# First tokens by quarters of the FFN units, with partial sums in SBUF; attention's element work on VectorE and ScalarE

## The chip, the core and the metric

The kernel runs on one core of one Trainium2 chip. The metric is the device time of one execution in microseconds; the runs' median is compared, and one execution was profiled.

## The reference, cut to what matters

An RWKV attention over batch 4, 8 heads, 768 steps, 48 channels a head; its output, as 3072 tokens of 384 features, goes through an RMS norm and a two-layer gated FFN with 1536 units:

```python
for t in range(S):
    cur = np.einsum('bhd,bhe->bhde', u[None] * kt, vt)
    y[:, :, t] = np.einsum('bhd,bhde->bhe', rt, state + cur)
    state = w[None, :, :, None] * state + np.einsum('bhd,bhe->bhde', kt, vt)
...
xn = x / rms * rms_g
g = xn @ w_gate
silu = g * (1.0 / (1.0 + np.exp(-g)))
return (silu * (xn @ w_val) @ w_out).astype(np.float32)
```

The three weight matrices come as 64-bit floats.

## The kernel before

The 768 steps are cut into 12 chunks of 64 steps; a chunk holds all four sequences, so 256 tokens. For each chunk `mixing` makes the attention: `prep` (L279 to L290) scales r and k into ME, MO and kc, multiplies r, k and u into rk, sums that to du and writes du on the diagonals of ME and MO; `prep_k` (L301) scales k into KH for the state; `scores` (L314) multiplies within the chunk and copies under a mask (L319); `states` (L371) and `outputs` (L337, L342) follow; `normalise` (L388 to L393) makes xT from yT and the sum sq of its squares (L350 to L355). rk, KH, the diagonals and the sums of sq are GpSimd's.

The FFN works on blocks of chunks, `blocks = [[0], [1], [2, 3], [4, 5], ...]`: products are 256 columns wide in the first two and 512 after. The 1536 units are 12 groups of 128, called units here (the index `nn`). `gate_val` multiplies a unit's gate and value weights with xT into two PSUM banks (L408), takes the sigmoid on ScalarE (L413) and two products on VectorE (L414, L415) to make h. `project` (L422) multiplies, for 128 tokens at a time, the h of all 12 units with w_out into one PSUM tile and ScalarE copies it out (L426).

The weights come in 24 pieces of 128x576. `stage` loads a raw piece (three buffers); `round_piece` makes the rounded 32-bit piece: one pass on ScalarE (ulp, L184), four on VectorE (mag, L186 to L191), of which L186 and L187 clamp small magnitudes, and an addition on GpSimd (L194). Pieces go in the order of all gate and value quarters, then all of w_out; a quarter is three units. `rounded(n)` makes a step wait in program order until n pieces are done.

The program is written as steps of the FFN with steps of the next block's mixing spread between them, and a scheduler then fixes one list per engine; each engine works through its list in order. All loads and stores are issued by SyncE (SP). At the end a count of decay values in range is read, and another, general path is taken if one was out of range.

## Time and profile before

| what | us |
|---|---|
| median of three runs | 766.51 (764.3 to 767.57) |
| the profiled execution's own time | 763.99 |
| its span, first to last instruction | 761.7 |
| TensorE busy in the span | 680.2 |
| VectorE, GpSimd, ScalarE busy | 338.9, 220.3, 154.9 |

The profile gives, for each engine, the busy time of its instructions. Engines work side by side, so the numbers don't add up to the span; what counts is which engine the others wait for in each stretch. PE is TensorE, DVE VectorE, ACT ScalarE, POOL GpSimd.

### The profile page before, as it was taken

The numbers are of one execution on the slowest core, as the hardware profiler recorded it, in microseconds if no ns is written. First come the engines' busy times: TensorE is split into PE (matmuls) and PEld (weight loads), VectorE is DVE, ScalarE is ACT, GpSimd is POOL, SyncE is SP. The second block draws the span as 40 slices with busy tenths as digits, with TensorE's granted clock in tenths as the row PEclk, the third lists the DMA queues.
The fourth block names the chain that finished last, engine by engine and source line by source line (L and its number), as shares of the span: only waits on it lengthen the run. The fifth ranks groups of instructions, "written<-read, shape, count | busy, mean of one in ns | idle before, by whom it ended". The sixth has DMA issues, their size and how long they took to land.

```text
span 761.7 us, 9960 instructions
## 1 busy us (share of the span) xinstructions
PE 680.2 (89%) x4238; PEld 389.6 (51%) x4238; DVE 338.9 (44%) x435; ACT 154.9 (20%) x307; POOL 220.3 (29%) x141
## 2 busy tenths in 40 slices
PE   2465667788999999999999999999999999999994
...
GB/s 230 169 49 163 236 76 197 130 42 78 100 41 30 16 75 53 99 11 42 72 8 52 99 11 42 78 0 64 100 0 1 1 1 22 22 0 0 1 21 27
DMA packets 13639, 46.85 MB, mean 62 GB/s; under 512 B 3216, under 2 KB 6288, under 8 KB 12432
## 3 DMA queue, kind: packets, MB, share of 16 engines
...
## 4 chain that ended last, share of the span: by engine, by line
PE 66%; POOL 13%; DVE 13%; issue 3%; DMA 3%; ACT 1%; POOLq 0%; ACTq 0%; DVEq 0%
PE pg L408 21%; PE pv L408 20%; PE po L422 17%; POOL KH L301 4%; DMA TOK<-in_tok_dram 3%; DVE xT L393 3%; PE pa L314 2%; PE pu L371 2%; POOL rk L285 2%; POOL rk L286 2%; DVE mag L191 2%; DVE mag L186 2%; PE py L337 1%; DVE mag L187 1%; PE py L342 1%
## 5 line engine op out<-in xcount | busy, mean ns | idle before, releaser
L408 PE MATMUL pg<-xT,wg 128*128 128x512 f32 (+1 forms) x504 | 210.6, 552 | 14.3 <-POOL wg L194 8.8
L408 PE MATMUL pv<-xT,wv 128*128 128x512 f32 (+1 forms) x504 | 203.4, 540 | 12.9 <-POOL wv L194 12.9
L422 PE MATMUL po<-wo,h 128*128 128x384 f32 x576 | 195.6, 495 | 12.3 <-POOL wo L194 10.3
L422 PEld LDWEIGHTS po<-wo,h 128*128 128x128 f32 x576 | 107.6, 191 | 87.0 <-POOL wo L194 12.6
L408 PEld LDWEIGHTS pv<-xT,wv 128*128 128x128 f32 x504 | 97.1, 194 | 104.6 <-issue 85.4
L408 PEld LDWEIGHTS pg<-xT,wg 128*128 128x128 f32 x504 | 96.6, 197 | 99.9 <-issue 69.4
L301 POOL TENSOR_TENSOR KH<-TOK,wk 64x768 f32<-64x768 f32 x22 | 47.0, 2137 | 244.0 <-PE pu L371 243.2
L414 DVE TENSOR_TENSOR h<-pg,h 128x512 f32<-128x512 f32 (+1 forms) x84 | 51.4, 612 | 145.1 <-ACT h L413 144.9
L413 ACT ACTIVATE h<-pg 128x512 f32<-128x512 f32 (+1 forms) x84 | 45.0, 536 | 287.7 <-PE pg L408 286.5
L415 DVE TENSOR_TENSOR h<-pv,h 128x512 f32<-128x512 f32 (+1 forms) x84 | 51.5, 613 | 70.0 <-PE pv L408 69.0
L426 ACT COPY o<-po 128x384 f32<-128x384 f32 x24 | 11.5, 478 | 194.5 <-PE po L422 140.7
L280 DVE TENSOR_TENSOR ME<-chan,up 48x1024 f32<-48x1024 f32 x12 | 18.5, 1543 | 61.1 <-PE py L342 61.1
L354 POOL TENSOR_TENSOR sq<-sq 128x256 f32<-128x256 f32 x12 | 17.0, 1419 | 89.6 <-ACT sq L350 89.6
L314 PE MATMUL pa<-ME,kc 48*64 48x64 f32 x384 | 30.3, 231 | 12.5 <-DVE kc L279 12.5
L314 PEld LDWEIGHTS pa<-ME,kc 48*64 48x64 f32 x384 | 26.3, 143 | 28.3 <-issue 13.8
L337 PE MATMUL py<-ME,VS 128*64 128x64 f32 x288 | 36.7, 231 | 2.5 <-DVE ME L319 2.0
L337 PE MATMUL py<-MO,VS 128*64 128x64 f32 x288 | 36.7, 231 | 1.5 <-DVE MO L319 1.5
L288 DVE TENSOR_REDUCE du<-rk 128x16 f32<-128x768 f32 x12 | 11.4, 951 | 57.0 <-POOL rk L286 57.0
L391 DVE RECIPROCAL rms<-rms 128x256 f32<-128x256 f32 x12 | 21.0, 1746 | 34.7 <-ACT rms L390 34.7
L342 PE MATMUL py<-MO,VS 128*48 128x64 f32 x288 | 36.2, 227 | 0.0
L342 PE MATMUL py<-ME,VS 128*48 128x64 f32 x288 | 36.2, 227 | 0.0
L393 DVE SCALAR_TENSOR_TENSOR xT<-yT,gcol,rms 128x256 f32<-128x256 f32 x36 | 33.4, 977 | 0.4
...
## 6 DMA issues: line engine op xcount, KB each, us to landing
...
raw<-in_wgt_dram SPq DMA_DIRECT2D x8, 576.0 KB, 4.1
raw<-in_wvl_dram SPq DMA_DIRECT2D x8, 576.0 KB, 4.5
raw<-in_wot_dram SPq DMA_DIRECT2D x8, 576.0 KB, 4.3
...
```

The lines of the kernel that those rows point to most:

```text
L280: nc.vector.tensor_mul(me[0:D], ch[0:D, 0], table(up[0:D]))
L301: nc.gpsimd.tensor_mul(KH[rows, z], TOK[rows, 1], free_dims(wk[rows], (0, B), (D, HP), (1, D)))
L314: nc.tensor.matmul(pa[to, bl, p, :], kc[rows, b, p, :], m[rows, b, p, :], start=True, stop=True, skip_group_check=True,)
L337: nc.tensor.matmul(py[64 * z : 64 * z + 64, i, cols], vs[:, z, b, at : at + L], m[:, b, 3, :], start=True, stop=False, skip_group_check=True,)
L342: nc.tensor.matmul(py[64 * z : 64 * z + D, i, cols], vs[:, z, b, i * D : (i + 1) * D], m[:, b, i, :], start=False, stop=True, skip_group_c ...
L391: nc.vector.reciprocal(rms, rms)
L393: nc.vector.scalar_tensor_tensor(out=xT[:, i, at : at + B * L], in0=yT_of[s][:, i], scalar=gcol[:, i : i + 1], in1=rms, op0=ALU.mult, op1= ...
L408: nc.tensor.matmul(ps_, wt[:, cc, o * P : (o + 1) * P], xT[:, cc, 0:nt], start=cc == 0, stop=cc == CC - 1)
L413: nc.scalar.activation(h, pg, AF.Sigmoid)
L414: nc.vector.tensor_mul(h, pg, h)
L415: nc.vector.tensor_mul(h, pv, h)
L422: nc.tensor.matmul(po, hT[blk, nn][:, j * P : (j + 1) * P], wo[i][:, o, :], start=nn == 0, stop=nn == NN - 1)
```

## The change

Chunks 0 to 3 go through the FFN one by one (256 columns), and chunks 0 to 2 by quarters: `cell(q, s)` makes units 3q to 3q+2 of chunk s and multiplies their h with that quarter of w_out. The first quarter's result is copied to SBUF by ScalarE, the later ones are added to it by VectorE. The pieces are ordered quarter by quarter, gate, value, out. From chunk 4 on there are blocks of two chunks as before. Attention's products rk, KH and the sums of sq are made by VectorE, the diagonals by 32 small ScalarE operations a chunk (chunk 0: four VectorE operations), and MO's lower half is a ScalarE copy of ME; ME and MO have one buffer instead of two. The PSUM pool `ps_at` has two banks instead of three, `ps_o` two instead of one. The clamp of small weights is gone from `round_piece`; instead `checks` loads every piece a second time and counts small magnitudes with two ScalarE passes, and the count decides on the general path at the end, together with the decay count.

```diff
-    ps_at = ctx.enter_context(tc.tile_pool(name="ps_at", bufs=3, space=PSUM))
-    ps_o = ctx.enter_context(tc.tile_pool(name="ps_o", bufs=1, space=PSUM))
+    ps_at = ctx.enter_context(tc.tile_pool(name="ps_at", bufs=2, space=PSUM))
+    ps_o = ctx.enter_context(tc.tile_pool(name="ps_o", bufs=2, space=PSUM))
...
+    ME = c_tile([P, B, HP, L], "ME")
+    MO = c_tile([P, B, HP, L], "MO")
...
+    pieces = [
+        (dst[i], src[i], k) for i in range(WQ) for dst, src in ((wg, wgt), (wv, wvl), (wo, wot)) for k in range(2)
+    ]
+    PER_Q = len(pieces) // WQ
+    queue, staged, state = deque(pieces), deque(), {"done": 0}
...
-            mag = raws.tile([P, CUT], FP32, name=f"mag_{n}", tag="mag", bufs=2)
+            bits = raws.tile([P, CUT], I32, name=f"bits_{n}", tag="bits", bufs=2)
             ulp = raws.tile([P, CUT], I32, name=f"ulp_{n}", tag="ulp", bufs=2)
             nc.scalar.activation(ulp, lo, AF.Copy, scale=2.0**-29)
-            mi = mag.bitcast(I32)
-            nc.vector.tensor_single_scalar(out=mi, in_=hi, scalar=0x7FFFFFFF, op=ALU.bitwise_and)
-            nc.vector.tensor_single_scalar(out=mag, in_=mag, scalar=2.0**-15, op=ALU.max)
             nc.vector.tensor_scalar(
-                out=mi, in0=mi, scalar1=3, scalar2=0x3FFFFFF8, op0=ALU.logical_shift_left, op1=ALU.bitwise_and
+                out=bits, in0=hi, scalar1=3, scalar2=0x3FFFFFF8, op0=ALU.logical_shift_left, op1=ALU.bitwise_and
             )
             nc.vector.scalar_tensor_tensor(
-                out=mi, in0=hi, scalar=-0x40000000, in1=mi, op0=ALU.bitwise_and, op1=ALU.bitwise_or
-            )
-            nc.gpsimd.tensor_tensor(out=dst.bitcast(I32), in0=mi, in1=ulp, op=ALU.add)
+                out=bits, in0=hi, scalar=-0x40000000, in1=bits, op0=ALU.bitwise_and, op1=ALU.bitwise_or
+            )
+            nc.gpsimd.tensor_tensor(out=dst.bitcast(I32), in0=bits, in1=ulp, op=ALU.add)
...
+    def checks(n):
+        _, src, k = pieces[n]
+        raw = raws.tile([P, CUT], I64, name=f"again_{n}", tag="raw")
+        nc.sync.dma_start(out=raw, in_=src[:, k * CUT : (k + 1) * CUT])
+        hi = raw.bitcast(I32).rearrange("p (n z) -> p n z", z=2)[:, :, 1].bitcast(FP32)
+        mag = raws.tile([P, CUT], FP32, name=f"mag_{n}", tag="ulp", bufs=2)
+        nc.scalar.activation(mag, hi, AF.Abs)
+        nc.scalar.activation(mag, mag, AF.Relu, scale=-(2.0**15), bias=1.0, accum_out=seen[:, n : n + 1])
...
-        nc.vector.tensor_mul(kc, ch[:, 1], table(down))
-        nc.vector.tensor_mul(me[0:D], ch[0:D, 0], table(up[0:D]))
-        nc.vector.tensor_mul(mo[64 : 64 + D], ch[64 : 64 + D, 0], table(up[64 : 64 + D]))
+        nc.vector.tensor_mul(ME, CH[:, 0], table(up))
+        nc.scalar.copy(MO[64:128], ME[64:128])
+        nc.vector.tensor_mul(kc, CH[:, 1], table(down))
         if s + 1 < NS:
             load_chan(s + 1)
+    def prep_u(s):
         rk = one.tile([P, B, HP, D], FP32, name=f"rk_{s}", tag="rk")
-        nc.gpsimd.tensor_mul(rk, TOK[:, 0], TOK[:, 1])
-        nc.gpsimd.tensor_mul(rk, rk, free_dims(utab, (0, B), (D, HP), (1, D)))
+        nc.vector.tensor_mul(rk, TOK[:, 0], TOK[:, 1])
+        nc.vector.tensor_mul(rk, rk, free_dims(utab, (0, B), (D, HP), (1, D)))
         du = work.tile([P, B * HP], FP32, name=f"du_{s}", tag="du")
         nc.vector.tensor_reduce(out=du, in_=rk.rearrange("p b h d -> p (b h) d"), op=ALU.add, axis=AX.X)
-        for t, rows in ((me, slice(64, 128)), (mo, slice(0, 64))):
-            nc.gpsimd.tensor_mul(
-                t[rows].rearrange("p b h t -> p (b h) t"),
-                free_dims(dmask[rows], (0, B * HP), (1, L)),
-                free_dims(du[rows], (1, B * HP), (0, L)),
-            )
+        for half in range(2):
+            for t, rows in ((ME, slice(64, 128)), (MO, slice(0, 64))):
+                if s == 0:
+                    nc.vector.tensor_mul(
+                        t[rows, 2 * half : 2 * half + 2].rearrange("p b h t -> p (b h) t"),
+                        free_dims(dmask[rows], (0, 2 * HP), (1, L)),
+                        free_dims(du[rows, 2 * HP * half :], (1, 2 * HP), (0, L)),
+                    )
+                    continue
+                for b in (2 * half, 2 * half + 1):
+                    for p in range(HP):
+                        x = b * HP + p
+                        nc.scalar.mul(t[rows, b, p, :], dmask[rows], du[rows, x : x + 1])
...
-            nc.gpsimd.tensor_mul(
+            nc.vector.tensor_mul(
                 KH[rows, z], TOK[rows, 1], free_dims(wk[rows], (0, B), (D, HP), (1, D))
...
-            nc.gpsimd.tensor_add(sq[:, 0], sq[:, 0], sq[:, 1])
-            nc.gpsimd.tensor_add(sq[:, 0], sq[:, 0], sq[:, 2])
+            nc.vector.tensor_add(sq[:, 0], sq[:, 0], sq[:, 1])
+            nc.vector.tensor_add(sq[:, 0], sq[:, 0], sq[:, 2])
...
+    def mixing(s, blk, at):
+        def last():
+            if at == 0:
+                xTs[blk] = work.tile([P, CC, 512], FP32, name=f"xT_{blk}", tag="xT", bufs=3)
+            normalise(s, xTs[blk], at)
+        def fourth():
+            outputs(s, 1)
+            states(s, 0)
+            states(s, 1)
+            if s + 2 < NS:
+                load_v(s + 2)
+        return [
+            lambda: prep_r(s), lambda: (prep_u(s), prep_k(s)), lambda: scores(s, 0), lambda: scores(s, 1),
+            lambda: outputs(s, 0), fourth, last,
+        ]
...
+    def project(blk, j, s, units, part=None):
+        rounded(PER_Q * ((units[-1]) // NQ + 1))
+        name = f"{blk}_{j}_{units[0]}"
+        po = ps_o.tile([P, DM], FP32, name=f"po_{name}", tag="po")
+        for nn in units:
             i, o = divmod(nn, NQ)
             nc.tensor.matmul(
-                po, hT[blk, nn][:, j * P : (j + 1) * P], wo[i][:, o, :], start=nn == 0, stop=nn == NN - 1
-            )
-        osb = work.tile([P, DM], FP32, name=f"o_{blk}_{j}", tag="o")
-        nc.scalar.copy(osb, po)
-        for bl in range(2):
-            row = (2 * (j % 2) + bl) * S + s * L
-            nc.sync.dma_start(out=out[row : row + L, :], in_=osb[bl * L : (bl + 1) * L, :])
-    blocks = [[0], [1]] + [[s, s + 1] for s in range(2, NS, 2)]
-    xTs = {}
-    def mixing(s, blk, at):
-        def first():
-            prep(s)
-            prep_k(s)
-        def third():
-            states(s, 0)
-            outputs(s, 0)
-        def fourth():
-            states(s, 1)
-            outputs(s, 1)
-            if s + 2 < NS:
-                load_v(s + 2)
-        def fifth():
-            if at == 0:
-                xTs[blk] = work.tile([P, CC, 512], FP32, name=f"xT_{blk}", tag="xT")
-            normalise(s, xTs[blk], at)
-        return [first, lambda: scores(s, 0), lambda: scores(s, 1), third, fourth, fifth]
-    load_v(1)
-    for f in mixing(0, 0, 0):
-        f()
-        round_piece()
-    for blk, chunks in enumerate(blocks):
-        nt = len(chunks) * B * L
-        ffn = [lambda nn=nn: gate_val(blk, nn, xTs[blk], nt) for nn in range(NN)]
-        ffn += [lambda j=j: project(blk, j, chunks[j // 2]) for j in range(nt // P)]
-        mix = []
-        if blk + 1 < len(blocks):
-            for x, s in enumerate(blocks[blk + 1]):
-                mix += mixing(s, blk + 1, x * B * L)
-        todo = deque(mix)
-        for x, f in enumerate(ffn):
+                po, hT[blk, nn][:, j * P : (j + 1) * P], wo[i][:, o, :], start=nn == units[0], stop=nn == units[-1]
+            )
+        if part in (None, 0):
+            osb = sums[blk, j] = work.tile([P, DM], FP32, name=f"o_{name}", tag="o", bufs=2 * FIRST)
+            nc.scalar.copy(osb, po)
+        else:
+            osb = sums[blk, j]
+            nc.vector.tensor_add(osb, po, osb)
...
+    def cell(q, s):
+        units = list(range(q * NQ, (q + 1) * NQ))
+        return [lambda nn=nn: gate_val(s, nn, B * L) for nn in units] + [
+            lambda j=j: project(s, j, s, units, q) for j in range(2)
+        ]
...
+    def alongside(steps, others, spare=0):
+        todo, n = deque(others), len(others)
...
+            due = n * (x + 1) // (len(steps) - spare)
...
+    first = mixing(0, 0, 0)
+    first[0]()
+    token_tables()
+    round_piece()
+    first[1]()
+    load_v(1)
+    for f in first[2:]:
+        f()
+        round_piece()
+    count = w_range()
+    rounded(PER_Q)
+    alongside(cell(0, 0), rounding(PER_Q))
+    alongside(cell(1, 0), mixing(1, 1, 0))
+    alongside(cell(0, 1) + cell(1, 1), rounding(PER_Q))
+    alongside(cell(2, 0) + cell(2, 1), mixing(2, 2, 0), 1)
+    alongside(cell(0, 2) + cell(1, 2) + cell(2, 2), rounding(PER_Q))
+    alongside(cell(3, 0) + cell(3, 1) + cell(3, 2), mixing(3, 3, 0), 2)
+    blocks = [[3]] + [[s, s + 1] for s in range(4, NS, 2)]
...
+        steps = block(chunks)
+        if x:
+            def checked(f):
+                f()
+                if again:
+                    checks(again.popleft())
+            steps = [lambda f=f: checked(f) for f in steps]
+        alongside(steps, mix, 1)
```

Three places in the engines' lists follow; a name's last numbers are the chunk or block and the unit or half (pg_0_2 is the gate product of unit 2 of block 0).

TensorE, after the first chunk's xT, before:

```order
L408 MATMUL pg_0_0_425<-xT_0_406,wg_0_118 128x256 x3
L408 MATMUL pv_0_0_426<-xT_0_406,wv_0_122 128x256 x2
L408 MATMUL pg_0_1_447<-xT_0_406,wg_0_118 128x256 x3
L408 MATMUL pv_0_1_448<-xT_0_406,wv_0_122 128x256
L408 MATMUL pg_0_2_469<-xT_0_406,wg_0_118 128x256 x3
L408 MATMUL pv_0_2_470<-xT_0_406,wv_0_122 128x256
L314 MATMUL pa_1_0_551<-ME_1_93,kc_1_491 64x64
```

and now:

```order
L450 MATMUL pg_0_2_457<-xT_0_394,wg_0_104 128x256 x3
L450 MATMUL pv_0_2_458<-xT_0_394,wv_0_108 128x256 x3
L468 MATMUL po_0_0_0_477<-wo_0_112,h_0_0_425 128x384
L468 MATMUL po_0_1_0_491<-wo_0_112,h_0_0_425 128x384
L468 MATMUL po_0_0_0_477<-wo_0_112,h_0_1_445 128x384
L468 MATMUL po_0_1_0_491<-wo_0_112,h_0_1_445 128x384
L468 MATMUL po_0_0_0_477<-wo_0_112,h_0_2_465 128x384
L468 MATMUL po_0_1_0_491<-wo_0_112,h_0_2_465 128x384
L450 MATMUL pg_0_3_513<-xT_0_394,wg_1_105 128x256 x2
L335 MATMUL pa_1_0_595<-ME_92,kc_1_525 64x64
```

The products with w_out (L468) of the first three units now stand behind these units; before, the second chunk's scores came next, and all products with w_out stood behind unit 11.

VectorE, while pieces are rounded (h_0_5 and h_0_6 are chunk 0's units), before:

```order
L187 TENSOR_SCALAR mag_10_541<-mag_10_541 128x576
L186 TENSOR_SCALAR mag_11_582<-raw_12_489 128x576
L188 TENSOR_SCALAR mag_10_541<-mag_10_541 128x576
L187 TENSOR_SCALAR mag_11_582<-mag_11_582 128x576
L191 SCALAR_TENSOR_TENSOR mag_10_541<-raw_13_467,mag_10_541 128x576
L188 TENSOR_SCALAR mag_11_582<-mag_11_582 128x576
L414 TENSOR_TENSOR h_0_6_600<-pg_0_6_592,h_0_6_600 128x256
L191 SCALAR_TENSOR_TENSOR mag_11_582<-raw_12_489,mag_11_582 128x576
L279 TENSOR_TENSOR kc_2_966<-chan_0_89,down_180 128x1024
L281 TENSOR_TENSOR MO_0_94<-chan_0_89,up_179 48x1024
L415 TENSOR_TENSOR h_0_6_600<-pv_0_6_593,h_0_6_600 128x256
```

and now, from the piece with number 12 on:

```order
L177 TENSOR_SCALAR bits_12_778<-raw_11_489 128x576
L180 SCALAR_TENSOR_TENSOR bits_12_778<-raw_11_489,bits_12_778 128x576
L177 TENSOR_SCALAR bits_13_804<-raw_10_503 128x576
L476 TENSOR_TENSOR o_0_0_0_481<-po_0_0_3_633,o_0_0_0_481 128x384
L180 SCALAR_TENSOR_TENSOR bits_13_804<-raw_10_503,bits_13_804 128x576
L476 TENSOR_TENSOR o_0_1_0_495<-po_0_1_3_667,o_0_1_0_495 128x384
L177 TENSOR_SCALAR bits_14_818<-raw_9_511 128x576
L180 SCALAR_TENSOR_TENSOR bits_14_818<-raw_9_511,bits_14_818 128x576
L375 TENSOR_TENSOR sq_1_664<-sq_1_664 128x256
L376 TENSOR_TENSOR sq_1_664<-sq_1_664 128x256
L290 TENSOR_TENSOR ME_92<-chan_89,up_170 128x1024
L292 TENSOR_TENSOR kc_2_920<-chan_89,down_171 128x1024
```

A piece has two rows where it had four (mag before, bits now); the additions of partial sums (L476) and the sums of sq (L375, L376) are new in the list, and ME is one operation over all 128 rows.

ScalarE, behind the last rounded piece (ulp_23), before:

```order
L184 ACTIVATE ulp_23_892<-raw_0_873 128x576
L426 COPY o_0_0_912<-po_0_0_899 128x384
L350 ACTIVATE sq_2_1103<-py_2_0_1077 128x3x128
L351 COPY yT_2_1102<-py_2_0_1077 128x3x128
L413 ACTIVATE h_1_2_990<-pg_1_2_982 128x256
L413 ACTIVATE h_1_3_1021<-pg_1_3_1013 128x256
L426 COPY o_0_1_938<-po_0_1_925 128x384
L413 ACTIVATE h_1_4_1052<-pg_1_4_1044 128x256
L413 ACTIVATE h_1_5_1114<-pg_1_5_1106 128x256
```

and now:

```order
L176 ACTIVATE ulp_23_1360<-raw_0_1289 128x576
L455 ACTIVATE h_0_6_904<-pg_0_6_896 128x256
L201 ACTIVATE mag_0_2291<-again_0_2289 128x576
L202 ACTIVATE mag_0_2291,seen_116<-mag_0_2291 128x576
L455 ACTIVATE h_0_7_916<-pg_0_7_908 128x256
L201 ACTIVATE mag_1_2308<-again_1_2306 128x576
L202 ACTIVATE mag_1_2308,seen_116<-mag_1_2308 128x576
L455 ACTIVATE h_0_8_934<-pg_0_8_926 128x256
L201 ACTIVATE mag_2_2331<-again_2_2329 128x576
L202 ACTIVATE mag_2_2331,seen_116<-mag_2_2331 128x576
L201 ACTIVATE mag_3_2388<-again_3_2386 128x576
```

The passes of `checks` (L201, L202), written beside the blocks from chunk 4 on, stand between the sigmoids of units 6 to 8 of chunk 0 and go on so to unit 6 of chunk 2. SyncE's list has their loads accordingly, right behind the last raw piece.

## Rows read from the trace of the kernel before

**Rows 1.** The page's busy line, and the slices of PE in tenths.
```profile
PE 680.2 (89%) x4238; PEld 389.6 (51%) x4238; DVE 338.9 (44%) x435; ACT 154.9 (20%) x307; POOL 220.3 (29%) x141
...
PE   2465667788999999999999999999999999999994
```

**Rows 2.** The table by stage: length, busy time of each engine, clock, DMA share, GB/s.
```profile
0.00:49.20 49.20, 17.34 (x234) 13.76 (x234) 35.42 (x52) 10.76 (x21) 42.58 (x38) 0.90 0.68 174
49.20:148.70 99.50, 69.34 (x532) 53.15 (x532) 91.12 (x135) 27.62 (x54) 50.35 (x31) 0.89 0.53 152
148.70:219.20 70.50, 65.03 (x532) 46.32 (x532) 33.01 (x41) 17.45 (x40) 38.39 (x22) 0.93 0.29 70
329.40:439.60 110.20, 109.43 (x693) 58.23 (x693) 44.30 (x49) 22.65 (x47) 28.71 (x16) 1.00 0.21 49
```

**Rows 3.** The chain in order of time, six of its pieces: start, length, what.
```profile
18.09 1.90 POOL rk L285
...
22.04 1.81 POOL rk L286
...
44.83 4.38 DVE xT L393 x3
...
329.44 1.98 PE pg L408 x4
...
656.56 2.57 PE pg L408 x6
...
743.95 8.02 PE po L422 x24
```

**Rows 4.** The timeline of VectorE and GpSimd, 62.6 to 65.7.
```profile
62.62 0.45 DVE L186 TENSOR_SCALAR mag<-raw 128x576 int32<-128x576 int32 x1
62.98 0.74 DVE L191 SCALAR_TENSOR_TENSOR mag<-raw,mag 128x576 int32<-128x576 int32 x1
...
63.87 1.49 POOL L194 TENSOR_TENSOR wg<-mag,ulp 128x576 int32<-128x576 int32 x1 [1.50 <-DVE mag L191]
64.02 0.41 DVE L415 TENSOR_TENSOR h<-pv,h 128x256 f32<-128x256 f32 x1
64.36 1.32 DVE L188 TENSOR_SCALAR mag<-mag 128x576 int32<-128x576 int32 x1
```

**Rows 5.** Groups of VectorE by shape: count, busy time, mean ns of one, idle before.
```profile
L393 DVE SCALAR_TENSOR_TENSOR xT<-yT,gcol,rms 128x256 f32<-128x256 f32 x36 | 33.4, 977 | 0.4
...
L391 DVE RECIPROCAL rms<-rms 128x256 f32<-128x256 f32 x12 | 21.0, 1746 | 34.7 <-ACT rms L390 34.7
...
L319 DVE COPY_PREDICATED ME<-mask,pa 64x512 f32<-64x512 int32 x24 | 17.6, 733 | 5.7 <-PE pa L314 5.4
...
L279 DVE TENSOR_TENSOR kc<-chan,down 128x1024 f32<-128x1024 f32 x12 | 15.0, 1249 | 0.6 <-DMA chan<-in_chan_dram 0.6
...
L288 DVE TENSOR_REDUCE du<-rk 128x16 f32<-128x768 f32 x12 | 11.4, 951 | 57.0 <-POOL rk L286 57.0
...
L414 DVE TENSOR_TENSOR h<-pg,h 128x256 f32<-128x256 f32 x24 | 10.0, 418 | 21.4 <-ACT h L413 21.4
```

**Rows 6.** Groups of GpSimd by shape.
```profile
L301 POOL TENSOR_TENSOR KH<-TOK,wk 64x768 f32<-64x768 f32 x22 | 47.0, 2137 | 244.0 <-PE pu L371 243.2
...
L286 POOL TENSOR_TENSOR rk<-rk,utab 128x768 f32<-128x768 f32 x12 | 22.0, 1834 | 0.9
```

**Rows 7.** Groups of ScalarE by shape.
```profile
L184 ACT ACTIVATE ulp<-raw 128x576 int32<-128x576 uint32 x24 | 17.6, 738 | 34.0 <-POOL wg L194 14.5 <-POOL wo L194 8.6 <-POOL wv L194 8.4
...
L379 ACT COPY VS<-pu 48x96 f32<-48x96 f32 x44 | 10.2, 231 | 0.0
```

**Rows 8.** The timeline of TensorE near 180, gate products of two units.
```profile
180.28 2.55 PE L408 MATMUL pg<-xT,wg 128*128 128x256 f32 x6
...
183.96 1.46 PE L408 MATMUL pg<-xT,wg 128*128 128x256 f32 x6
```

**Rows 9.** DMA issues by line: count, KB each, median us to landing.
```profile
raw<-in_wgt_dram SPq DMA_DIRECT2D x8, 576.0 KB, 4.1
```

More of the change, by code (lines that the diff above doesn't have):

```diff
@@ new lines, in w_range, with prep_r @@
+    def w_range():
+        inr = c_tile([P, HP], "inr")
+        nc.vector.tensor_scalar(out=inr, in0=wraw, scalar1=W_LOW, scalar2=None, op0=ALU.is_ge)
+        inr2 = c_tile([P, HP], "inr2")
+        nc.vector.scalar_tensor_tensor(out=inr2, in0=wraw, scalar=W_HIGH, in1=inr, op0=ALU.is_le, op1=ALU.mult)
+        count = c_tile([P, 2], "count")
+        nc.vector.tensor_reduce(out=count[:, 0:1], in_=inr2, op=ALU.add, axis=AX.X)
+        return count
+    kc_of, du_of = {}, {}
+    def prep_r(s):
@@ L312, in scores @@
             for p in range(HP):
[L313 removed]
+                for rows, to, m in ((slice(0, D), slice(64, 128), ME), (slice(64, 64 + D), slice(0, 64), MO)):
                     nc.tensor.matmul(
@@ new lines, in project, with block @@
+        if part in (None, WQ - 1):
+            for bl in range(2):
+                row = (2 * (j % 2) + bl) * S + s * L
+                nc.sync.dma_start(out=out[row : row + L, :], in_=osb[bl * L : (bl + 1) * L, :])
+    FIRST = 3
+    def cell(q, s):
[3 more added lines that the diff above has]
+        ]
+    def block(chunks):
+        blk, nt = chunks[0], len(chunks) * B * L
+        return [lambda nn=nn: gate_val(blk, nn, nt) for nn in range(NN)] + [
+            lambda j=j: project(blk, j, chunks[j // 2], list(range(NN))) for j in range(nt // P)
+        ]
@@ L476, in fast @@
+    def alongside(steps, others, spare=0):
+        todo, n = deque(others), len(others)
+        for x, f in enumerate(steps):
+            f()
+            due = n * (x + 1) // (len(steps) - spare)
+            while todo and n - len(todo) < due:
                 todo.popleft()()
```

138 lines of the change are left out of this document (64 added, 74 removed).

## The prediction

> **What bounds the kernel now.** I read the busy line and the slices first [rows 1]: TensorE (PE) is busy 680.2 of 761.7 us, but the slices say where it is not: 2 to 8 tenths in the first ten slices, 9 in nearly all that follow. A table by stage makes this exact [rows 2]. The stage 329.4 to 439.6 is the steady state (one block of two chunks with 512-column products): PE 109.4 of 110.2 us at granted clock 1.00. Nothing on another engine can shorten that. The stage 49.2 to 148.7, in which the weights are rounded, has PE busy 69.3 of 99.5 us and VectorE (DVE) 91.1: DVE sets its length. Before 49.2, the end of the first chunk's xT (44.83 + 4.38, [rows 3]), GpSimd (POOL) is busy 42.6 us and PE 17.3.
>
> So the program falls in two parts. The chain in order of time [rows 3] gives the seam: the first product of block [4,5] starts at 329.44. From there to the end is 432.3 us, all PE, and the last block, without attention beside it, takes from 656.56 to 751.97, 95.4 us: 47.7 for one chunk's two layers. The steady block's 110.2 less 95.4 leaves 14.8 for the attention of two chunks, 7.4 each. Up to the seam PE must do, after the first xT, four chunks' layers and five chunks' attention: 4 x 47.7 + 5 x 7.4 = 228 us. Before it has 329.4 - 49.2 = 280 for them. The 52 us between, and the first 49, are all there is to gain.
>
> **The change part by part.** Everything ahead of the seam is re-cut; behind it the products and their order stay, so I keep the 432.3.
>
> *First chunk.* In the chain [rows 3] POOL works without a break from the first rk at 18.09 to the end of the second at 23.85 with one KH between, after another KH step. Now rk and KH are on DVE, one of the two rk ahead of everything. The path loses some 6 us of POOL, and about 2 of the 4.38 that three xT took (2.9 at their mean of 0.98, [rows 5]), and six clamps of 0.45 in front of it; it gains two KH on DVE, near 1 each, and a VectorE wait for TOK at the start. I take 9 us off: xT ends at 40.
>
> *Stage B, from that xT to the first h of unit 6.* The order of VectorE shows 100 instructions there. Priced: 20 weight pieces, now two operations in place of four, 0.45 + 0.74 each [rows 4], 23.8; 25 products h at 0.42, 10.5; 8 masked copies at 0.73, 5.8; three kc and one ME at 1.25, 5.0; three du 2.9; a reciprocal 1.75; three xT 2.9 [rows 5]; two sq additions at h's 0.42, 0.8. New on DVE are six rk and four KH: no row shows them there. From below, kc's 1.25 cut from 1024 to 768 columns is 0.94; from above, POOL's own 1.83 to 2.14 [rows 6]. I take 0.94, since kc is the same operation on the same engine: 9.4 (up to 10 more in the range). The four additions of partial sums, 128x384 out of PSUM, lie above h's 0.42 for 256 columns: 0.55 each, 2.2. Together 65. Each starts about 0.08 before the one ahead ends (62.98 against 62.62 + 0.45, [rows 4]): less 8, 57.
>
> To this come the waits for POOL. A tensor_scalar that takes 0.45 alone took 1.32 at 64.36, while POOL added the piece it had started at 63.87 (1.49 long); the product h at 64.02, which reads PSUM, went through beside it in 0.41 [rows 4]. In the new order there stand 20 such POOL additions; behind each, h products and masked copies cover about half a microsecond on average before the next operation with SBUF inputs alone. So 20 x 1.0 = 20. Of before's 8.4 us of idle DVE [rows 2] part was waiting for rk on POOL, which is gone: I leave 5. Stage B: 57 + 20 + 5 = 82. PE's own work in it is four quarters of 11.9 and 1.3 chunks of attention, 57: DVE stays the bound. PE may run two units (5 us) ahead at its end.
>
> *Stage C, to unit 8 of chunk 2.* PE: five quarters and one attention, 59.6 + 7.4 = 67. The order of ScalarE (ACT) and SyncE (SP) shows that all 24 range tests (`checks`), written for the late blocks, were moved here: each loads a piece again and runs two passes on ACT between the sigmoids. One pass over 128x576 was 0.74 [rows 7], so 24 x 1.48 = 35.5. The diagonals, formerly two POOL operations, are now 32 small ACT operations per chunk; nothing in the trace is 64x64. The nearest row, 48x96, is 0.23 [rows 7]; less 32 columns I take 0.20, 6.4 a chunk, some 40 of them in C, 8. The rest of ACT's work ran at 27.6 of 99.5 us [rows 2], here 19. Sum 62 of 67: covered, though with little left over. If it were not covered, sigmoids would wait, then h, then the PSUM banks that PE writes.
> The Trainium skill, "VectorE: DVE Perf Modes", section on the TRN2 errata, speaks against many small operations: a ScalarE operation from SBUF pays a fixed 224 cycles besides its columns. An estimate by that page is (224 + 64)/1.2 = 240 ns for each, 7.7 us a chunk; C's sum would be 64, still covered. No row of this trace shows which holds.
> The loads: 24 pieces of 576 KB land in 4.1 us each [rows 9], three buffers in flight, so about 1.4 us each at best; not the limit unless they run singly (below).
>
> *Stage D, to the seam.* The last quarters of chunks 0 to 2 and chunk 3, with the rest of the attention: 228 - 57 - 67 = 104 us of PE.
> Around mixing, PE waits a little: between 148.7 and 219.2, with two chunks' mixing beside 256-column products, it idles 5.5 us [rows 2]. I give C and D 3 each. The 256-column form costs nothing itself: six passes take 1.46 at the full clock [rows 8], six of 512 2.57 [rows 3]. Single ME/MO, and two instead of three `ps_at` banks, are covered in the steady state by 5 us of product per unit; uncovered, a bank waits for two ACT evictions, about 1 us a chunk.
>
> *Sum.* 40 + 82 - 5 + 67 + 3 + 104 + 3 = 294 for the seam; + 432.3 = 726; + 2.3, what the profiled execution has around its span (763.99 against 761.7), = 728.5. The runs' median is 2.5 above the profiled one: **731**.
>
> **Rivals.**
> *VectorE no longer bounds B.* If POOL's waits fall into idle time, B is PE's 57 and nothing waits: 40 + 228 + 432.3 + 2.3 + 2.5 = 705. For it: the order interleaves PSUM readers. Against: DVE's 57 alone leaves no slack, and any POOL wait adds.
> *B stays as long as before.* PE, ACT and DVE hand over to each other within three-unit cells; if each hand-over is exposed, fewer operations give nothing and B is 99.5 again: 731 + 17.5 = 748. For it: the order puts pieces of the next quarter ahead of the first chunk-1 h. Against: DVE idled only 8% before.
> *The lower clock.* Six passes took 2.55 at 180.28, after a wait, and 1.46 at 183.96 [rows 8]: half the clock. If all of B ran at the lower level, PE's 57 would be 114, 37 over the 77 it has: 768, no gain. Against: before, PE idled there too, and the clock was still 0.89 [rows 2], about a fifth of the time low, which makes 57 some 70. The Trainium skill, "TensorE: Matmul & The Clock Gate", section HAM oscillation, states that waits between bursts send the array back to 1.2 GHz; by that rule this rival would hold, and the granted clock of B will tell.
> *The tests run singly: slower.* If SP issues each reload only when ACT has read the one before, each test costs a landing and a pass, 4.1 + 0.74; 24 make 116 against C's 70: 731 + 46 = 777. It eats the whole gain from 4.4 us a test on (35 us over 24 tests, on top of 70/24). For it: the sigmoids stand between the tests in ACT's list, so all PE work of C waits with them. Against: three buffers.
>
> **How the numbers follow.** Forecast 0.56; PE-bound B 0.12; B as before 0.20; the clock 0.05; single tests 0.05; 0.02 for a loss in the steady part. 0.5% (4 us) is about what a measurement of this kernel can tell from no change. Faster: forecast, PE-bound, B as before, 0.88; same 0.06 (the clock, near 768, and half of the last); slower 0.06. The dear end of rk and KH makes 741. The range takes in PE-bound at 704 and B-as-before with a few us, 755, and leaves the last two out. The likeliest case's own range is 718 to 742.
>
> **What would show it.** Right: a seam (first 512-column product of block 4) near 294 with 432 behind it; in B DVE busy over 90%, with tensor_scalar means well above 0.45; 24 tests inside some 70 us from unit 6 on; granted clock 0.85 to 0.95 in B. Wrong: ACT at its full share in C with PE idle behind sigmoids; the stretch behind the seam longer than 432 by PE waits on `ps_at`; rk or KH near 2 us on DVE; an xT that ends later than 45.

## The result, and the profile after

The kernel after takes 720.1 us (median of 4 runs, 718.8 to 721.3), the one before 766.1 beside it: a ratio of 0.940, interval 0.937 to 0.943. Forecast were 731 with a range of 704 to 755. The gain is 46 us, 11 more than forecast. The profiled execution took 719.5, its span 717.8. Two executions far from all others, one of e5 (810.6 us, at a granted clock of 0.84) and one of the kernel before beside e9 to e11 (2457.6 us), are left out of the medians below.

The page of the kernel after, busy line and slices, against [rows 1]:

```profile
PE 669.5 (93%) x4382; PEld 414.0 (58%) x4382; DVE 323.7 (45%) x494; ACT 290.6 (40%) x763; POOL 46.4 (6%) x42
...
PE   2378798899999999999999999999999999999995
...
DVE  6797978372325674444622444632433420322200
ACT  3365484898127365406326106425205501211000
POOL 7123333000000000000000000000000000000000
PEclk9979799999999999999999999999999999999998
```

PE's slices stay at 8 or 9 from the sixth on, and at 9 from the ninth (144 us), where before it was the eleventh (190 us). POOL lost 174 us of work, ACT gained 136, and neither number is the gain. The table by stage, against [rows 2] (length, then busy time of PE, PEld, DVE, ACT, POOL, each with its instructions, granted clock, DMA share, GB/s), with stages A (to the first xT), B, C, D as forecast, then the blocks from the seam on:

```profile
0.00:40.25 40.25, 13.71 (x234) 11.29 (x234) 29.79 (x57) 16.50 (x32) 17.51 (x22) 0.91 0.80 207
...
40.25:118.40 78.15, 67.36 (x489) 51.71 (x490) 68.58 (x99) 44.86 (x117) 26.24 (x19) 0.89 0.69 199
118.40:182.00 63.60, 60.94 (x441) 47.94 (x440) 30.12 (x56) 54.76 (x136) 2.67 (x2) 0.97 0.80 252
182.00:291.60 109.60, 108.82 (x966) 83.77 (x965) 55.80 (x95) 53.49 (x164) 0.00 (x0) 1.00 0.31 68
...
291.80:400.90 109.10, 109.10 (x693) 58.39 (x693) 45.13 (x60) 40.33 (x113) 0.00 (x0) 1.00 0.24 57
...
617.40:717.80 100.40, 92.88 (x243) 45.34 (x241) 16.74 (x25) 10.84 (x18) 0.00 (x0) 0.97 0.05 11
```

The first xT ends at 40.25 (forecast 40). B takes 78 us (82). From there to the seam it is 173 (172: the 177 of C and D less the 5 that PE runs ahead), and the seam comes at 291.6 (294). Behind it lie 426.2 us, where 432 were forecast.

What PE waits for in the stage in which the weights are rounded (engine and line, releaser: us in all, times, longest), first before, from 49.2 to 148.7, then after, in B:

```profile
PE pv L408 <- POOL wv L194: 12.9, 6, 3.9
PE pg L408 <- POOL wg L194: 8.8, 3, 7.2
PE po L422 <- POOL wo L194: 5.3, 5, 1.8
```

```profile
PE po L468 <- DVE h L457: 2.6, 2, 2.4
PE pg L450 <- POOL wg L183: 2.5, 1, 2.5
PE po L468 <- POOL wo L183: 2.4, 2, 1.8
PE pm L407 <- DVE sq L376: 1.7, 1, 1.7
```

Before, PE stood 27.0 us for pieces that POOL had to add; after, 4.9. But an addition is only the last link of a piece. What POOL itself waits for, before, from 49.2 to 148.7:

```profile
POOL wo L194 <- DVE mag L191: 18.0, 7, 3.7
POOL wv L194 <- DVE mag L191: 14.2, 6, 3.8
POOL wg L194 <- DVE mag L191: 7.1, 5, 1.5
```

For 39.3 us of this stage POOL stood with an addition at the head of its list and waited for VectorE, which was busy for 91.1 of the 99.5 us [rows 2]. So the prediction's reading, that VectorE sets the length of this stage, agrees with the waits.

### The profile page after: what moved, and what is told of

Its sections match the earlier page's. It is cut to its first block, busy times and chain, and to the rows that moved or that the text cites. A ratio compares the mean times of both kernels' runs of the same rounds, so it can differ in the third digit from the quotient of the medians.

```text
span 717.8 us, 10714 instructions
## 1 busy us (share of the span) xinstructions
PE 669.5 (93%) x4382; PEld 414.0 (58%) x4382; DVE 323.7 (45%) x494; ACT 290.6 (40%) x763; POOL 46.4 (6%) x42
## 4 chain that ended last, share of the span: by engine, by line
PE 80%; DVE 7%; ACT 4%; DMA 3%; issue 3%; POOL 2%; DVEq 0%; POOLq 0%; ACTq 0%
PE pg L450 24%; PE po L468 23%; PE pv L450 23%; PE pa L335 3%; PE py L358 2%; PE py L363 2%; PE pu L392 2%; DMA again<-in_wvl_dram 1%; DVE bits L180 1%; DVE bits L177 1%; DMA chan<-in_chan_dram 1%; DMA again<-in_wgt_dram 1%; ACT mag L201 1%; DVE kc L292 1%; ACT ME L315 1%
## 5 line engine op out<-in xcount | busy, mean ns | idle before, releaser
L450 PE MATMUL pg<-xT,wg 128*128 128x256 f32 (+1 forms) x576 | 209.8, 499 | 8.6 <-DVE xT L412 6.1
L450 PE MATMUL pv<-xT,wv 128*128 128x256 f32 (+1 forms) x576 | 203.6, 490 | 0.1
L468 PE MATMUL po<-wo,h 128*128 128x384 f32 x576 | 194.8, 491 | 5.1 <-DVE h L457 2.6
L468 PEld LDWEIGHTS po<-wo,h 128*128 128x128 f32 x576 | 108.1, 191 | 77.7 <-DVE h L457 5.7
L455 ACT ACTIVATE h<-pg 128x256 f32<-128x256 f32 (+1 forms) x96 | 46.8, 487 | 228.6 <-PE pg L450 228.1
L456 DVE TENSOR_TENSOR h<-pg,h 128x256 f32<-128x256 f32 (+1 forms) x96 | 53.4, 557 | 144.5 <-ACT h L455 144.4
L457 DVE TENSOR_TENSOR h<-pv,h 128x256 f32<-128x256 f32 (+1 forms) x96 | 53.4, 557 | 60.8 <-PE pv L450 59.0
L315 ACT ACTIVATE MO<-dmask,du 64x64 f32<-64x64 f32 x176 | 47.7, 338 | 23.4 <-PE py L363 21.0
L315 ACT ACTIVATE ME<-dmask,du 64x64 f32<-64x64 f32 x176 | 44.8, 332 | 0.6
L358 PEld LDWEIGHTS py<-ME,VS 128*64 128x64 f32 x288 | 29.6, 145 | 18.9 <-issue 17.3
L335 PEld LDWEIGHTS pa<-ME,kc 48*64 48x64 f32 x384 | 27.1, 148 | 16.6 <-issue 10.6
L290 DVE TENSOR_TENSOR ME<-chan,up 128x1024 f32<-128x1024 f32 x12 | 14.7, 1224 | 47.5 <-PE py L363 46.3
L335 PE MATMUL pa<-MO,kc 48*64 48x64 f32 x384 | 30.0, 236 | 0.0
```

Of the source, the lines that this page charges most:

```text
L290: nc.vector.tensor_mul(ME, CH[:, 0], table(up))
L315: nc.scalar.mul(t[rows, b, p, :], dmask[rows], du[rows, x : x + 1])
L335: nc.tensor.matmul(pa[to, bl, p, :], kc[rows, b, p, :], m[rows, b, p, :], start=True, stop=True, skip_group_check=True,)
L358: nc.tensor.matmul(py[64 * z : 64 * z + 64, i, cols], vs[:, z, b, at : at + L], m[:, b, 3, :], start=True, stop=False, skip_group_check=True,)
L450: nc.tensor.matmul(ps_, wt[:, cc, o * P : (o + 1) * P], xT[:, cc, 0:nt], start=cc == 0, stop=cc == CC - 1)
L455: nc.scalar.activation(h, pg, AF.Sigmoid)
```

## Experiments

The prediction's theory: the gain comes from VectorE, whose list bounds the rounding stage and gets shorter. Rival 1: the quarters do it, which give PE work on few pieces. Rival 2: POOL's list does it, in which attention work stands between the additions of pieces. All results (us; seam: first 512-column product of block [4,5]; "under before": median against the median of the kernel before on the same chip):

| kernel | first xT ends | seam | behind seam | median | under before |
|---|---|---|---|---|---|
| before | 49.2 | 328.2 | 433.5 | 766.1 | |
| after | 40.3 | 291.6 | 426.2 | 720.1 | 46.0 |
| e1 before, two po banks | 52.8 | 327.2 | 431.2 | 761.5 | 4.8 |
| e2 after, one po bank | 38.9 | 293.0 | 426.9 | 720.7 | 45.6 |
| e3 after, no tests | 39.3 | 289.8 | 428.3 | 720.0 | 46.2 |
| e4 after, no addition | 36.7 | 281.7 | 426.1 | 707.4 | 58.9 |
| e5 after, four operations | 39.2 | 302.2 | 426.1 | 729.2 | 36.7 |
| e6 after, work on POOL | 44.5 | 301.5 | 426.1 | 730.5 | 35.4 |
| e7 after, whole chunks | 40.3 | 294.1 | 425.9 | 721.3 | 44.6 |
| e8 before, two operations | 48.3 | 312.3 | 435.1 | 751.4 | 14.5 |
| e9 after, rounding without POOL | 38.6 | 289.0 | 426.1 | 717.3 | 49.6 |
| e10 before, both moves | 39.2 | 291.5 | 429.8 | 723.2 | 43.7 |
| e11 after, neither move | 48.1 | 315.7 | 426.3 | 741.8 | 25.0 |
| e12 as e9, diagonals on VectorE | 38.6 | 290.5 | 426.2 | 715.0 | 52.5 |

The intervals of the ratios are about 0.2 to 0.4% to either side, 1.5 to 3 us.

**e1 and e2: the banks.** e1 is the kernel before with this edit, e2 the kernel after with its reverse:

```diff
-    ps_at = ctx.enter_context(tc.tile_pool(name="ps_at", bufs=3, space=PSUM))
-    ps_o = ctx.enter_context(tc.tile_pool(name="ps_o", bufs=1, space=PSUM))
+    ps_at = ctx.enter_context(tc.tile_pool(name="ps_at", bufs=2, space=PSUM))
+    ps_o = ctx.enter_context(tc.tile_pool(name="ps_o", bufs=2, space=PSUM))
```

> The kernel before, with one thing changed: two PSUM banks for po and two (not three) for the attention. Theory A (the second po bank is the gain behind the seam): the PE waits for ACT's copy of o vanish, each steady block takes 109.1 in place of 110.2 us, the last 92.8 in place of 95.4, behind the seam 426 in place of 432; the whole 766 becomes 759 to 761. Rival B (that gain comes from the re-cut attention work or the end of the program): behind the seam stays at 431 to 433, the whole 765 to 767. Rival C (two attention banks hold PE up in the early stages): the seam moves back by 2 us or more and eats the gain.

> The kernel after with one po bank and three for the attention, as before. Theory A: behind the seam 426 becomes 430 to 432; ahead of it each of the 16 pairs of partial projections waits for the copy or addition of the first, about 0.6 us each where PE is the bound, so the seam moves from 292 to 296 to 302; the whole 720 becomes 728 to 736. Rival B (the partial sums wait in idle time of PE): only the stretch behind the seam grows, the whole 724 to 726.

The chain of waits shows the last block's projections, in e1 first, then in e2; the kernel after reads as e1:

```profile
718.19 30.97 PE po L422 x96
```

```profile
680.06 7.75 PE po L468 x24
688.37 8.02 PE po L468 x24
696.94 8.02 PE po L468 x24
705.56 8.02 PE po L468 x24
```

With two banks the four projections run without a gap; with one they start 8.3 to 8.6 us apart, as before [rows 3]. From its first product to its last projection the last block takes 92.9 us in e1 and after, 95.5 in e2 and before: the bank is worth 2.6 us. The steady blocks don't care: 110.5 in e1, 108.9 in e2. e1's median, 761.5, lies just above A's range and well below B's. In e2 A's 4 to 10 us ahead of the seam failed: of the pairs of partial projections only two show up in PE's waits, 1.7 us in all, and the median is that of the kernel after, below both theories. In its profile an end that came 1.3 us sooner after the last projection, and 0.6 in the steady blocks, make up for most of the 2.6. That end takes 9.3 to 9.9 us in the five kernels without the late tests (before, e1, e3, e8, e10) and 6.3 to 7.7 in the nine with them, one trace each; why was not shown.

**e3: no tests.**

```diff
-    again = deque(range(len(pieces)) if wide else [])
+    again = deque()
```

> The kernel after without the range tests of the weights: 24 reloads of 576 KB and 48 ACT passes with their accumulator reads are left out (the output is the same for weights in range). Theory A (the tests are covered in stage C): PE's 2.7 us of idle time in 118 to 178 and some clock are all there is to gain, the seam 289 to 291, the whole 717 to 720. Rival B (ACT, busy 51.6 of 59.6 us there, holds back the sigmoids and with them PE): the seam 6 to 10 us earlier, the whole 710 to 714.

A held: the seam 1.8 us earlier, the median the same, since the end took 2.1 us more (9.7 against 7.6). The groups of ACT in the kernel after, from 118 to 184:

```profile
L201 ACT ACTIVATE mag<-again 128x576 f32<-128x576 f32 x24 | 17.5, 733 | 7.1 <-DMA again<-in_wgt_dram 2.0 <-DMA again<-in_wvl_dram 1.7 <-POOL wo L183 1.7
L202 ACT ACTIVATE mag<-mag 128x576 f32<-128x576 f32 x24 | 16.3, 680 | 0.5
...
L202 ACT ACTIVATION_READ_ACCUMULATOR mag<-mag 128x1 f32 x24 | 4.5, 189 | 0.0
L315 ACT ACTIVATE MO<-dmask,du 64x64 f32<-64x64 f32 x16 | 4.2, 336 | 0.0
```

A test is 1.60 us, forecast 1.48: the sum of a pass is read out by an instruction of its own, 0.19 us. All 24 ran in these 64 us and waited only some 5 us for their loads, so they did not run singly.

**e4 and e5: VectorE's rounding made lighter and heavier.** e4 leaves out ulp and the addition (first diff); e5 puts mask and clamp back (second):

```diff
-            nc.scalar.activation(ulp, lo, AF.Copy, scale=2.0**-29)
...
-            nc.gpsimd.tensor_tensor(out=dst.bitcast(I32), in0=bits, in1=ulp, op=ALU.add)
```

```diff
+            nc.vector.tensor_single_scalar(out=bits, in_=hi, scalar=0x7FFFFFFF, op=ALU.bitwise_and)
+            nc.vector.tensor_single_scalar(out=mag, in_=mag, scalar=2.0**-15, op=ALU.max)
```

> The kernel after without the rounding of the last bits: 24 ACT passes (ulp) and 24 POOL additions are left out, VectorE writes the weights itself (they are cut off at 20 bits of mantissa). Theory A (VectorE bounds stage B, POOL's additions lengthen its operations): in B tensor_scalar falls from a mean of 0.79 to 0.45 us and scalar_tensor_tensor from 0.94 to 0.75, VectorE's busy time from 68.6 to 57; B falls from 78 to 67 to 70 us, the whole to 708 to 712. Rival B (PE's own work at its lower clock, 67 us, and the hand-overs bound B): the operations get shorter all the same, but B stays at 75 or more, the whole 716 to 720.

> The kernel after with the two operations on VectorE put back ahead of each weight piece (mask and clamp, 128x576, 0.45 us each alone, 0.62 to 0.73 in the rows of before). Theory A (VectorE bounds stage B): 20 pieces in B add 18 to 26 us to its 68.6 us, of which some 5 fall into its idle 9.6; B 78 becomes 91 to 99, the first xT 2 to 4 us later, the whole 720 becomes 736 to 746. Rival B (PE's own 67 us and hand-overs bound B, VectorE has room): 724 to 729.

VectorE's rounding groups (mean in ns after the busy us) for the 20 pieces of B, in the kernel after (40 to 120), then in e4 (36 to 108; the second group is split there by what it writes, and the eight pieces of wo are shown):

```profile
L180 DVE SCALAR_TENSOR_TENSOR bits<-raw,bits 128x576 int32<-128x576 int32 x20 | 18.8, 940 | 0.2
L177 DVE TENSOR_SCALAR bits<-raw 128x576 int32<-128x576 int32 x20 | 15.7, 785 | 1.1 <-POOL wg L183 1.1
```

```profile
L175 DVE TENSOR_SCALAR bits<-raw 128x576 int32<-128x576 int32 x20 | 9.0, 451 | 1.5 <-DMA raw<-in_wvl_dram 0.9 <-DMA raw<-in_wot_dram 0.7
L178 DVE SCALAR_TENSOR_TENSOR wo<-raw,bits 128x576 int32<-128x576 int32 x8 | 6.0, 747 | 0.0
```

And B as a whole, in e4 and in e5:

```profile
36.65:105.65 69.00, 64.94 (x489) 50.69 (x489) 56.69 (x96) 30.17 (x97) 0.00 (x0) 0.91 0.75 220
```

```profile
39.17:126.18 87.01, 68.89 (x417) 50.76 (x416) 79.38 (x128) 43.61 (x116) 31.36 (x19) 0.85 0.60 175
```

e4 came out as A had it, with a median of 707.4, just under A's 708; VectorE's busy time of 56.7 is the 57 that the sum had without POOL's waits. In e5 B grew by 8.9 us with 10.8 more of VectorE, and the median is 729.2, just past rival B's 729 and far from A's 736. The rounding operations take 48.9 us of VectorE there, 33.0 in the kernel after; some 5 us of its other work slid behind the first h of unit 6. Both look like a stage bound by VectorE. But e4 took 24 passes off ACT as well; e9 separates the two.

**e6 and e7: the two halves of the change undone in the kernel after.** e6 puts rk, KH, the sums of sq and the diagonals on `nc.gpsimd`; e7 orders pieces and blocks as before:

```diff
-    alongside(cell(0, 0), rounding(PER_Q))
...
-    alongside(cell(3, 0) + cell(3, 1) + cell(3, 2), mixing(3, 3, 0), 2)
-    blocks = [[3]] + [[s, s + 1] for s in range(4, NS, 2)]
+    alongside(block([0]), [f for g in mixing(1, 1, 0) for f in (round_piece, round_piece, g)] + rounding(10), 1)
+    alongside(block([1]), mixing(2, 2, 0) + mixing(3, 2, B * L), 1)
+    blocks = [[s, s + 1] for s in range(2, NS, 2)]
```

> The kernel after with the attention's element work (rk, KH, the sums of sq, the diagonals) on POOL again, as before; ME and MO stay single. Theory A (the move is worth a few us at three places): first xT 40 becomes 45 to 48 (rk and KH at 1.8 to 2.1 on POOL in place of 0.95), B about as long (VectorE loses 9 us of work but is lengthened by POOL's), each steady block 109.1 becomes 110.2 (PE waits for sq on POOL, as before); the whole 726 to 733. Rival B (it moved from one covered place to another): 718 to 722. Rival C (with single ME and MO the products wait for POOL's diagonals): steady blocks over 111, the whole above 735.

> The kernel after with the first chunks in the order of before: gate and value pieces ahead of all output pieces, blocks of whole chunks [0], [1], [2, 3] and so on, no quarters and no partial sums; two-operation rounding, element work, banks and late tests as after. Theory A (the operation count on VectorE did it, not the quarters): the rounding stage of before loses its 28.5 us of mask and clamp and gains 9.4 of rk and KH, so it ends near 120 and the seam comes at 292 to 300; the whole 720 to 728. Rival B (the quarters give PE work while pieces are rounded): PE starves behind the pieces, the whole 735 to 745.

e6 is A's size at other places: the first xT 4.3 us later, and in PE's waits up to the seam

```profile
PE pg L450 <- DVE xT L412: 11.9, 4, 8.5
```

where the kernel after has 1.2; the steady blocks stay at 109.1, so that part of A fell. e7 is A: without any quarter the kernel is 1.4 us slower, within the noise. So rival 1 falls where both moves are made. What the quarters are worth without the moves was not run.

**e8, e10, e11: the moves alone, and the order alone.** e8 takes the two lines of mask and clamp out of the kernel before; e10 also has, in the kernel before,

```diff
-        nc.gpsimd.tensor_mul(rk, TOK[:, 0], TOK[:, 1])
+        nc.vector.tensor_mul(rk, TOK[:, 0], TOK[:, 1])
...
+            for x in range(B * HP):
+                nc.scalar.mul(t[rows, x // HP, x % HP, :], dmask[rows], du[rows, x : x + 1])
```

KH and the sums of sq are moved in the same way. Neither e8 nor e10 has the late tests of small weights, which a kernel for use would need (by e3 they cost nothing in the kernel after). e11 is the kernel after with the edits of e5 and e6 together.

> The kernel before with two-operation rounding (mask and clamp of small weights left out), nothing else changed. Theory A (the clamps on VectorE bound the stage 49 to 149): VectorE's 91.1 us there become 63, the stage 75 to 80 long, the first xT 2 to 3 us earlier, the whole 766 becomes 740 to 746. Rival B (the hand-overs between engines and the order of pieces bound it): less than 10 us, 756 or more.

> The kernel before with both engine moves of the change and nothing of its order: two-operation rounding (mask and clamp of small weights left out), and rk, KH and the sums of sq on VectorE, the diagonals on ACT. Theory A (the two moves add up as measured one by one, 14.5 and 10.4 us): 738 to 745, so that some 16 us of the whole gain lie in the set-up order, the cutting of the mixing steps and the banks. Rival B (VectorE, the bound of the stage, gets 9 us of work more and loses what the two operations saved): 748 to 756. Rival C (the moves are all there is besides banks): 725 to 732.

> The kernel after with both engine moves undone: mask and clamp back ahead of each weight piece, and rk, KH, sums of sq and diagonals on POOL; quarters, set-up order, steps of the mixing, banks and late tests stay. Theory A (the two add up as measured one by one, 9.6 and 10.4 us): 737 to 743. Rival B (they cover each other: one of the two already sets the bound): 730 to 734. Rival C (VectorE's longer list and POOL's slow down each other): 747 or more.

e8 misses its A by 5 us. From 48.3 to 160 PE still waits for POOL there:

```profile
PE pg L406 <- POOL wg L192: 7.0, 6, 3.2
PE pm L386 <- POOL sq L353: 4.9, 1, 4.9
PE po L420 <- POOL wo L192: 4.2, 5, 1.8
PE pv L406 <- POOL wv L192: 2.0, 5, 0.6
```

e10 was better than its best case: 43.7 of the 46 us come without the new order. Its seam, 291.5, is that of the kernel after, its steady blocks take 108.8, and what it lacks behind the seam is the second po bank (its last block takes 95.6) and some of the end. But PE waits no less for POOL's additions than in e8. From 39.2 to 160:

```profile
PE po L424 <- POOL wo L192: 6.1, 6, 1.5
PE pv L410 <- POOL wv L192: 6.0, 5, 2.2
PE pg L410 <- POOL wg L192: 4.7, 2, 4.0
```

That is 16.8 us, against 13.2 in e8, so rival 2 does not hold as it was put. What the move took away is attention work of POOL's: on the chain of work that ended last POOL has 14% in e8, 9 of them KH and rk, and 4% in e10 (a share of the chain is not yet a price):

```profile
PE 66%; POOL 14%; DVE 9%; DMA 5%; issue 4%; ACT 1%; POOLq 0%; ACTq 0%; SPq 0%; DVEq 0%
PE 83%; DVE 6%; POOL 4%; issue 3%; ACT 2%; DMA 1%; POOLq 0%; ACTq 0%; DVEq 0%
```

In the profiles e10 is 26.1 us shorter than e8: 9.1 up to the first xT, 5.6 from there to the last rounded piece, 6.2 from there to the seam, 5.3 behind it. Part of it is TensorE's clock, which no theory named: the mean granted clock is 0.985 to 0.988 in the runs of e10, 0.969 to 0.974 in those of e8, and 0.977 to 0.980 in those of the kernel after. From the first xT to the last rounded piece it is 0.95 in e10 and 0.85 in e8, with PE idle for about 18 us in both.

On the other side e11, with neither move, still has 25.0: A's sum of e5 and e6 holds there. So in before's order the element work is worth 43.7 - 14.5 = 29.2 on top of the two operations, in after's order 10.6. Moves and order overlap: PE's idle time from the first xT to the seam is 36.2 us before, 18.2 in e10, 28.0 in e11 and 14.2 after. Which part of the order (quarters, set-up, the cutting of the mixing steps, banks) gives e11 its 25.0 was not separated.

**e9 and e12: the addition without POOL.** ACT writes three bits as 16-bit halves into words whose upper half is set once; VectorE does the rest:

```diff
+            nc.scalar.activation(low, lo, AF.Copy, scale=0.93 * 2.0**-29)
+            nc.vector.scalar_tensor_tensor(
+                out=bits, in0=hi, scalar=3, in1=ulp, op0=ALU.logical_shift_left, op1=ALU.bitwise_xor
+            )
+            nc.vector.scalar_tensor_tensor(
+                out=dst.bitcast(I32), in0=hi, scalar=-0x80000000, in1=bits, op0=ALU.bitwise_and, op1=ALU.bitwise_or
+            )
```

e12 adds to that the diagonals of every chunk on VectorE:

```diff
-                if s == 0:
+                if True:
```

> The kernel after with the weights rounded without POOL: ACT writes the three low bits, 0 to 7, as 16-bit halves into words whose upper half is set once, VectorE shifts and combines in two scalar_tensor_tensor operations and writes the weight itself. The rounding saturates at 7 in place of carrying (an error of up to about one unit of the last place), and holds for weights under 2, so the range tests get one more operation each on VectorE (a maximum over 128x576). Theory A (the 12 us of the run without the addition come from POOL's work beside VectorE's): 20 pieces x (0.75 + 0.75) make 30 us on VectorE in place of 34.5 in the rows of after, and xT, kc and sq shorten too; B 69 to 73 in place of 78, the whole 708 to 713. Rival B (the gain came from the work left out itself, ACT's ulp passes and the wait for them): 716 to 722.

> The kernel of the run before without POOL in the rounding (two scalar_tensor_tensor operations and the 16-bit halves, saturating at 7), with the diagonals of every chunk on VectorE, as chunk 0 has them, in place of 32 ACT operations. Theory A (ACT's list is the bound that came up: 16.7 of its 45.5 us in B are diagonals, and VectorE's masked copies wait 6.4 us for them): VectorE gets 4 x 0.69 us more per chunk, B 70 to 74 in place of 78, the whole 709 to 714. Rival B (ACT's wait for the raw pieces to land, 8.6 us ahead of sigmoids in its list, stays and bounds B): B 76 to 78, the whole 715 to 719.

B of e9, and what VectorE waits for in it:

```profile
38.58:116.55 77.97, 69.21 (x438) 52.94 (x438) 59.59 (x95) 45.47 (x117) 0.00 (x0) 0.86 0.68 198
```

```profile
DVE h L463 <- ACT h L462: 5.3, 5, 1.5
DVE ME L347 <- ACT ME L322: 4.7, 2, 2.9
DVE bits L179 <- ACT ulp L178: 3.2, 5, 1.4
```

A fell: VectorE has 9 us less to do than in the kernel after, and B is as long as there, 78.0. Its idle time went from 9.6 to 18.4, most of it behind ACT, whose list has ulp passes that wait for raw pieces to land (8.6 us), ahead of sigmoids and diagonals. So e4's 12.9 us did not come from POOL's additions alone: without them, but with the ACT passes, e9 gains 3.6 over the kernel after. e12 takes 16.7 us of diagonals off that list: the first h of unit 6 comes at 112.95, B is 74.4, just over A's 74. The profiled execution lost this again by the seam, with PE waiting 5.3 us for ACT's copy yT (1.3 in e9), but at 718.8 it was the slowest of the five; the median of 715.0 is the lower end of rival B. It remains the fastest kernel here whose weights keep all their bits, to about one unit of the last place: 0.931 of before, interval 0.929 to 0.934.

## Why the prediction was nearly right

*First chunk.* 40.25 against 40. rk and KH on VectorE take 0.93 to 0.95 us; the lower of the two bounds was right. The element work is worth 8.9 of the 9 us with the clamps in place (48.1 in e11, 39.2 in e5) and 4.3 without (e6); in e10 both moves in the old set-up order end xT at 39.2, so the new order adds nothing. Single traces with the same set-up differ by up to 3.6 us here (49.2 before, 52.8 in e1).

*Stage B.* 78 against 82. The 57 us of VectorE held (56.7 in e4). "20 x 1.0" for POOL's additions was too much: the busy time of 68.6 less 57.0 leaves 11.6, 0.58 each. "I leave 5" for idle time was too little: 9.6. That these two errors partly cancel is luck. The timeline of the kernel after, first POOL, then VectorE, shows what an addition does:

```profile
47.27 1.41 POOL L183 TENSOR_TENSOR wo<-bits,ulp 128x576 int32<-128x576 int32 x1 [7.30 <-DVE bits L180]
50.67 1.48 POOL L183 TENSOR_TENSOR wo<-bits,ulp 128x576 int32<-128x576 int32 x1 [1.99 <-DVE bits L180]
```

```profile
47.38 1.62 DVE L177 TENSOR_SCALAR bits<-raw 128x576 int32<-128x576 int32 x1
...
50.82 0.41 DVE L456 TENSOR_TENSOR h<-pg,h 128x256 f32<-128x256 f32 x1
51.15 1.62 DVE L180 SCALAR_TENSOR_TENSOR bits<-raw,bits 128x576 int32<-128x576 int32 x1
```

The tensor_scalar that begins beside an addition ends at 49.00, 0.32 after it; the product h, which reads PSUM, goes through. The Trainium skill, "Trainium Architecture — The Big Picture", section "What this means for kernel authors", calls the port pair that VectorE and GpSimd share an exclusive lock and not a split of bandwidth; these rows agree. The mean is 0.58 because of the 19 additions that start in B 14 hold up one operation of VectorE, by 0.3 to 1.3 us; beside the other five ran only products, masked copies or du, or nothing.

"DVE stays the bound" was half right, and the sign "busy over 90%" came out at 88. e4 and e5 move B by 9 us either way, but e9 shows that VectorE does not bound it alone: with 9 us less there, ACT's list and PE's own work keep B as long. That work is busy for 67 us at the granted clock of 0.89, which is that of the stage before; by the clock's record it is 59.5 at the full clock, where the sum had 57.

*Stages C and D.* 173 against 172 from the first h of unit 6. PE's lead was 2.4 us and not 5: its first product of unit 6 starts at 116.0, and from there to the seam it is 175.6 against 177. The tests were covered, as priced (e3); for the diagonals no run of the kernel after shows it, and in e12 B gets 3.6 us shorter without them. The diagonals step at 0.24 us and not 0.20 (eight in 2.02 us, each 0.334 long). The 240 ns that the prediction worked out from the Trainium skill, "VectorE: DVE Perf Modes", section on the TRN2 errata, agree with this step.

*Behind the seam.* This is the step that failed: "behind it the products and their order stay, so I keep the 432.3". Both stayed, and it is still 426. (The chain's 329.44 lies 1.3 us behind the first product of the block; from that, at 328.2, the stretch was 433.5 before, so 7.3 us are to be explained.) The second po bank, priced at nothing, is worth 2.6 in the last block, where nothing else is there for PE while ACT copies. The three steady blocks lost 2.6 together (109.1, 109.1, 107.4 for 110.4, 109.8, 108.0): before, PE waits some 0.7 us a block there, for sq on POOL and for xT. Either the element work off POOL in the old steps removes that (e10), or the new steps with the work on POOL (e6). The last 2.1 are the program's end, which is shorter in every kernel that has the late tests; no run shows why. Besides, from the span to the runs' median it is 2.3 us and not the 4.8 of the sum.

*The rivals.* Of the four, none came: B was neither 57 nor 99 us, the clock was at its lower level for some 17 of B's 78 us as the stage before had led to expect, and the tests overlapped. What no rival said is that the quarters are not needed once both moves are made (e7), and that POOL's attention work holds up more than the first chunk: the sum took 9 us off there, most of it for this move, and counted 9.4 us more of VectorE in B; e10 over e8 shows a gain of 29.2. The number could be right without that, because behind B the sum counts PE's own work, and the moves and the order each lead there.

What stays open: kernel e10 with a second po bank, by its rows some 720 us without any of the new order, was not run. Open too are how much of e10's 29.2 us is the clock, what the quarters give without the moves, and why the end is shorter with the tests.
